# Sketched attention and a GELU layer: the opening in another order

## Chip, cores and metric

The kernel runs on one core of a Trainium2 chip. The metric is the device time of one launch, in microseconds (us). Five engines work beside each other and meet at semaphores: TensorE (PE, matmuls; PEld is its weight load), VectorE (DVE), ScalarE (ACT), GpSimd (POOL) and SyncE (SP, which here issues nearly all transfers).

## What is computed

The reference has two parts. For each of 4 batches and 4 heads, with 1088 tokens of width 32, queries and keys get 64 features each: the products of 8 by 8 sketch values.

```python
def phi(x):
    a = np.einsum('rd,bhsd->bhsr', S1, x)
    b = np.einsum('rd,bhsd->bhsr', S2, x)
    return np.einsum('bhsi,bhsj->bhsij', a, b).reshape(*x.shape[:-1], r * r)
q_p, k_p = (phi(q), phi(k))
kv = np.einsum('bhsf,bhsd->bhfd', k_p, v)
z = np.sum(k_p, axis=2)
num = np.einsum('bhsf,bhfd->bhsd', q_p, kv)
den = np.einsum('bhsf,bhf->bhs', q_p, z)[..., None] + 1e-06
...
h = x @ w_in                                   # x: 4352 x 128, w_in: 128 x 2048
g = 0.5 * h * (1.0 + erf(h * inv_sqrt2))
return (g @ w_out).astype(np.float32)          # w_out: 2048 x 128
```

The quotient num / den, with its heads side by side, is x. The sketches S1 and S2 and the weights w_in and w_out come as 64-bit floats.

## The kernel before, in words

**Tiling.** The 1024 main tokens of a batch make two chunks of 512; the 64 tokens that remain of each batch make one last chunk of 256. There are 9 chunks, numbered from 0. The hidden layer of a chunk is 16 hidden products (`hidden`, L564: 128 rows of w_in by 512 tokens), each followed by a GELU on ScalarE (L571), and then output products with w_out. A 512-column product in 32-bit floats shows as two matmul records of 0.43 us each. The first 8 of the 16 hidden blocks of chunks 0 and 1 use a plain output product (`project`, L692); all later ones use a form with fewer multiplications (`two_products`, L641), for which GpSimd makes sums.

**Order.** The order of instructions on each engine is that of the program's text; nothing reorders it (the loop at the end of the function makes each instruction depend on the one before it on its engine). So an instruction that waits holds up everything behind it on its engine. The opening is written out by hand (L724 to L792). Behind it a loop runs over steps t: step t issues one hidden product, then what `at(t, ...)` has put into its slot, then the output products that are due (`products[t]`, two steps behind their hidden product). Steps 0 to 3 are hidden blocks 0 to 3 of chunk 0, steps 4 to 7 those of chunk 1, then blocks 4 to 7 of each.

**The opening's work for batch 0.**

- *Sketches* (`sketches`, L292): SR, the rounded sketches, is transposed on TensorE (L294). VectorE makes S12 (L295) and sT (L297) of it, GpSimd Srep (L300).
- *Keys*: eight TensorE transposes (L306, `key_turn`), copied by ScalarE to kT (L308); key products with S12 (L350); feature products k_p (L367 on VectorE, L364 on GpSimd, of a copy a_t).
- *The remainder keys*: one transpose (`key_turn_rem`), one product (L374), a copy a_rem on ScalarE (L378), and k_p_rem on VectorE (L379).
- *kv*: `kv_first` (L405) sums over the main tokens, `kv_sum_rem` (L425) adds the remainder. ScalarE copies the sum (kv_T, L431), TensorE transposes it (L435), ScalarE copies it to kz (L439).
- *Queries of chunk 0*: VectorE transposes q (L453). Those of chunk 1: TensorE (L306), with the copy on ScalarE put off (L763). Then per chunk `expand_products` (L462), four `expand_copy` on ScalarE (A_sb, L469) and two `expand_multiply` of two instructions each on VectorE (q_pT, L483).
- *Numerators and denominators of chunks 0 and 1* (`attend_by_token`): small products (L530), then on VectorE denominators (L535), reciprocal (L536) and quotient (x_tok, L538). `turn_x` transposes x_tok on TensorE (L546) and copies it to xT, one half on ScalarE and one on VectorE (L549). xT is what the hidden products read.

**Rounding of weights.** Class `Rounding` makes 32-bit floats of the 64-bit words, piece by piece (pieces end at columns 256, 512, 1024, 1536 and 2048): `low_words` (L250, ScalarE), `fields` (L254 and L256, VectorE), `exponents` (L262, ScalarE), `mantissas` (L270 on VectorE; or L267 on ScalarE and L268 on GpSimd), `signs` (L275, VectorE), `product` (L280, VectorE or GpSimd). `finish` is mantissas, signs and product on VectorE. The tiles in between are taken in turn from pools with two or three buffers each.

**Idle products.** `keep_busy` (L722) issues products of zeros whose result nobody reads.

**Transfers.** SP issues the loads one by one, in the order of the text: keys 0 (two halves), queries 0, values 0 (two halves), key remainders, w_in's first piece, the value remainder, queries 1, two more pieces of weights. The rest (`load_rest`) waits for a one-word memset on GpSimd (L167).

Of the kernel before, what the change touches and what calls it, by code (L numbers as in the profile page):

```python
# [8 lines left out]
FP = mybir.dt.float32  # L9
# [7 lines left out]
def kernel(  # L17
# [56 lines left out]
    def halves(banks):  # L74
        return [banks[:, i] for i in range(2)]

    def hidden_bank():
        return hps.tile([128, CW], FP, name="h_ps")

    def out_bank():  # L80
        return ops.tile([128, CW], FP, name="o_ps")
# [4 lines left out]
    LC = 512  # L86
# [10 lines left out]
    def load_main(eng, n, b, heads=slice(0, H)):  # L97
        eng.dma_start(out=main[n, b][:, heads],
                      in_=src_of[n][b, heads, 0:MAIN, :].rearrange("h (p j) d -> p h j d", j=J))
# [18 lines left out]
    def load_rem(n, b):  # L118
        sp.dma_start(out=rem[n][b // 2 * REM:(b // 2 + 1) * REM, b % 2],
                     in_=src_of[n][b, :, MAIN:S, :].rearrange("h p d -> p h d"))  # L120
# [36 lines left out]
    def load_w_in(i):  # L157
        src, e = words(moe_w_in)
        c0, c1 = pieces[i]
        sp.dma_start(out=landing(w_in_sb[i], e == 2), in_=src[:, c0 * e:c1 * e])  # L160
# [17 lines left out]
    for r in range(2):  # L178
        load_main(sp, "k", 0, slice(r, H, 2))
    load_q(0)  # L180
    for r in range(2):
        load_main(sp, "v", 0, slice(r, H, 2))
    load_rem("k", 0)
    load_rem("k", 2)
    load_w_in(0)
    load_rem("v", 0)
    load_q(1)
# [3 lines left out]
    def load_rest():  # L191

        load_w_out(1, gated=True)
        for i in range(2, len(pieces)):
            load_w_in(i)
            load_w_out(i)
        for b in range(1, B):
            load_turned_k(b)
            load_main(sp, "v", b)
            for c in range(NCH):  # L200
                load_q(b * NCH + c)
            if b == 1:
                for n, b1 in (("k", 1), ("k", 3), ("v", 1), ("v", 2), ("v", 3)):
                    load_rem(n, b1)
        for b in range(B):
            load_rem("q", b)
# [29 lines left out]
    class Rounding:  # L236


        def __init__(self, dst):
            self.dst, self.wide = dst, dst.name in raw  # L240
            if self.wide:
                rows, n = dst.shape
                self.lo, self.hi = raw[dst.name][:, :, 0], raw[dst.name][:, :, 1]
                self.a, self.e, self.r = (mlp.tile([128, LC], U32, name=f"bits_{x}", bufs=2 if x == "r" else 3)[:rows, :n]
                                          for x in "aer")
                self.low, self.m = (mlp.tile([128, LC], FP, name=f"bits_{x}")[:rows, :n] for x in ("low", "m"))

        def low_words(self):
            if self.wide:
# [42 lines left out]
    def sketches():  # L292
        ps = work_bank()
        pe.transpose(ps[:, :2 * R], in_=SR, identity=ident[:2 * R, :2 * R])  # L294
        dve.tensor_mul(out=S12, in0=ps[:, None, :2 * R].broadcast_to([128, H, 2 * R]),  # L295
                       in1=mask4[:, :, None].broadcast_to([128, H, 2 * R]))
        dve.tensor_copy(out=sT, in_=ps[:, :2 * R])  # L297
        for i in range(2):
            src = sT[:, 0:R, None] if i == 0 else sT[:, None, R:2 * R]
            pool.tensor_copy(out=Srep[:, i], in_=src.broadcast_to([128, R, R]))  # L300

    def transposed(ps, name, srcs, copy):

        n = len(srcs) * 128
        for i, s in enumerate(srcs):
            pe.transpose(ps[:, i * 128:(i + 1) * 128], in_=s, identity=ident)  # L306
        t = att.tile([128, n], FP, name=name, bufs=1 if name == "kT_rem" else 2)
        copy(out=t, in_=ps[:, :n])  # L308
        return t

    def four_tokens(n, b, h, c):
        return main[n, b][:, h, c * JC:(c + 1) * JC, :].rearrange("p j d -> p (j d)")
# [12 lines left out]
        for r in range(2):  # L325
            pool.tensor_copy(out=to[rows, :, r, r, :], in_=rem["v"][rows, b % 2, r::2])

    def key_turn(b, r, ps, copy):
        kT[r] = transposed(ps, "kT", [four_tokens("k", b, h, c) for h in (r, r + 2) for c in range(NCH)], copy)

    def key_turn_blocks(b, r):

# [37 lines left out]

        kT["rem"] = transposed(ps[:, 256:], "kT_rem", [rem["k"][:, pair].rearrange("p h d -> p (h d)")], copy)

    def key_features_rem(pair, ps):
        pe.matmul(ps[:, 384:448], lhsT=kT["rem"][:, :128], rhs=S12.rearrange("p h r -> p (h r)"), start=True, stop=True)  # L374
        k_p_rem[pair] = big.tile([128, H, R, R], FP, name=f"k_p_rem{pair}")
        ab = ps[:, 384:448].rearrange("p (h r) -> p h r", r=2 * R)
        a = att.tile([128, H, R], FP, name="a_rem")
        act.copy(out=a, in_=ab[:, :, 0:R])  # L378
        dve.tensor_mul(**spread(k_p_rem[pair], a, ab[:, :, R:2 * R]))  # L379

# [52 lines left out]
    def turn_kv(b, ps, copy):  # L433
        if b == 0:
            pe.transpose(ps[:, :128], in_=kv_T[b], identity=ident)  # L435
        else:
            for rows in (slice(0, 64), slice(64, 128)):
                pe.matmul(ps[rows, :128], lhsT=kv_T[b][:, rows], rhs=ident, start=True, stop=True)
        copy(out=kz[b].rearrange("p c n -> p (c n)"), in_=ps[:, :128])  # L439
# [280 lines left out]
    def keep_busy(n, ps, cols=256):  # L720
        for i in range(n):
            pe.matmul(ps[:, CW - cols:], lhsT=idle[:, 0:128], rhs=idle[:, :cols], start=True, stop=True)  # L722
# [6 lines left out]
    r.exponents()  # L729
    r.finish()  # L730
    key_turn(0, 0, hidden_bank(), by_act)
    key_turn(0, 1, hidden_bank(), by_act)
    sketches()
    keep_busy(1, bank)
    query_turn(0)
    widen_v(0)
    banks = [out_bank(), out_bank()]
# [2 lines left out]
    widen_v(1)  # L740
    widen_v_rem(0)
    expand_products(0)
    w_in = [Rounding(w) for w in w_in_sb[:2]]
    key_turn_rem(0, banks[1], by_dve)
    w_in[0].fields()
    for g in range(2):
        expand_copy(0, g)
    expand_multiply(0, 0)
    kv_bank = out_bank()
    kv_first(kv_bank, 0)  # L750
    expand_copy(0, 2)
    key_features_rem(0, banks[1])
    expand_copy(0, 3)
    expand_multiply(0, 1)
    kv_first(kv_bank, 1)
    keep_busy(1, hidden_bank())
    kv_sum_rem(0, kv_bank)
    w_in[0].exponents()
    take_kv(0, kv_bank, by_act)
    late = []  # L760
    query_turn(1, lambda **a: late.append(a))
    turn_kv(0, kv_bank, by_act)
    by_act(**late[0])  # L763
    w_in[0].signs()
    w_in[1].fields()
    w_in[0].low_words()
    w_in[0].mantissas(by_pool=True)
    load_rest()
    w_in[0].product(pool)
    w_in[1].low_words()  # L770
    w_in[1].exponents()
    banks = [hidden_bank(), hidden_bank()]
    keep_busy(1, banks[0], 128)
    w_out = [Rounding(w) for w in w_out_sb[:2]]
    w_out[0].fields()
    attend_by_token(0, banks)
    expand_products(1)
    bank = out_bank()
    keep_busy(1, bank)
    w_out[0].low_words()  # L780
    for g in range(2):
        expand_copy(1, g)
    w_in[1].mantissas()
    w_in[1].signs()
    w_in[1].product(pool)
    turn_x(0, [hidden_bank(), hidden_bank()])
    keep_busy(1, bank)
    for i in range(2):
        for g in range(2):
            if i:  # L790
                expand_copy(1, 2 + g)
        expand_multiply(1, i)  # L792


    steps = [(n, fi) for f in range(0, USUAL, 4) for n in range(NCH) for fi in range(f, f + 4)]
# [3 lines left out]
    def at(t, f, *a):  # L799
        slots[t].append(lambda: f(*a))  # L800
# [61 lines left out]
    at(17, features_rem, 1)  # L862
    at(18, channel_sums, 4)
    at(18, query_expand, 2)
    at(20, finish_keys, 1)
    at(22, lambda: turn_kv(1, held["kv"], by_act))
    at(23, query_turn, 3)
    at(24, attend, 2)
    for i, t in enumerate((25, 26, 28)):
        at(t, channel_sums, i)  # L870
    for n in range(3, NCHUNK):
# [49 lines left out]
    for t in range(len(steps) + LAG):  # L921
        if t < 4:

            hidden(0, t)
            if t == 0:
                w_out[0].exponents()
                w_out[0].finish()
                w_out[1].fields()
            if t == 3:
                attend_by_token(1, halves(work_banks()), lambda: (w_out[1].exponents(), w_out[1].low_words(),  # L930
                                                                  w_out[1].mantissas(by_pool=True)))
                w_out[1].signs()
                w_out[1].product()
                for u in range(4):
                    for f, *a in products[u]:
                        f(*a)
            continue
        if t == 4:
            turn_x(1, [work_bank(), work_bank()])
            for f, *a in products[t]:  # L940
                f(*a)
        for n in drains[t]:
            drain(n)
        if t < len(steps):
            n, fi = steps[t]
            hidden(n, fi, by_halves=t >= 18 and (n < NMAIN or fi < 5))
        if t < len(steps) and steps[t][0] < NMAIN and steps[t][1] % NB == NB - 1:
            n, b = steps[t][0], steps[t][1] // NB
            if b >= first_block(n):
                token_sums(n, b)  # L950
        for f in slots[t]:
            f()
        for n in done[t]:
            store(n)
        if t != 4:
            for f, *a in products[t]:
                f(*a)
    for n in done[len(steps) + LAG]:
# [40 lines left out]
```

## Time and profile before

| | us |
|---|---|
| median of 4 runs | 274.21 (273.63 to 274.26) |
| the profiled execution, its own time | 273.63 |
| its span in the profile | 271.8 |
| TensorE / VectorE / ScalarE / GpSimd busy | 265.7 / 167.2 / 145.8 / 170.6 |
| hidden products (L564), busy | 140.7 |
| first hidden product of chunk 0 starts | 17.43 |
| first hidden product of chunk 1 starts | 25.67 |
| longest stop of TensorE after that, before L396 | 0.91, ending at 55.41 |

The span is the time from the first instruction of the profile to the last; the execution's own time is longer by what lies around it. Lines such as "L564" are lines of the kernel before, and "x8" counts instructions. The profile's timeline merges neighbours of one kind: its second number runs from the start of the first to the end of the last. The chain that ended last is followed back from the end of the program, at each step to what released the instruction. A matmul's end is modelled, so I go by starts, and by the distance from one start to the next. "Issue" is time in which an engine waited for nothing that the profile shows.

### The profile page before, as it was taken

The numbers are of one execution on the slowest core, as the hardware profiler recorded it, in microseconds if no ns is written. First come the engines' busy times: TensorE is split into PE (matmuls) and PEld (weight loads), VectorE is DVE, ScalarE is ACT, GpSimd is POOL, SyncE is SP. The second block draws the span as 40 slices with busy tenths as digits, with TensorE's granted clock in tenths as the row PEclk, the third lists the DMA queues.
The fourth block names the chain that finished last, engine by engine and source line by source line (L and its number), as shares of the span: only waits on it lengthen the run. The fifth ranks groups of instructions, "written<-read, shape, count | busy, mean of one in ns | idle before, by whom it ended". The sixth has DMA issues, their size and how long they took to land.

```text
span 271.8 us, 5822 instructions
## 1 busy us (share of the span) xinstructions
PE 265.7 (98%) x2326; PEld 137.0 (50%) x2326; DVE 167.2 (62%) x264; ACT 145.8 (54%) x291; POOL 170.6 (63%) x176
## 2 busy tenths in 40 slices
PE   8999999989999999999999999999999999999994
PEld 6755444354454545444445445344444454445794
DVE  5996778543795699679316898488047902760140
ACT  4694766566655633583357533773367344734431
POOL 3331006899987499368875798568866886777400
PEclk9999999999999999999999999999999999999999
DMA  7459373635201100010200000200200020011020
GB/s 211 156 153 364 60 173 65 171 71 144 53 2 18 24 0 2 16 27 0 42 0 2 0 2 2 39 0 2 39 0 2 0 40 4 1 22 19 2 38 20
DMA packets 37915, 13.50 MB, mean 50 GB/s; under 512 B 28288, under 2 KB 37248, under 8 KB 37888
## 3 DMA queue, kind: packets, MB, share of 16 engines
q1 hardware_dynamic: 37648, 13.05, 19.3%
q8 instruction: 18, 0.29, 0.4%
q10 hardware_dynamic: 240, 0.08, 0.1%
q14 instruction: 9, 0.07, 0.1%
HBM read 10.90 MB, written 2.23 MB: 48 GB/s over the span
## 4 chain that ended last, share of the span: by engine, by line
PE 94%; DVE 3%; ACT 2%; issue 0%; POOL 0%; POOLq 0%
PE h_ps L564 43%; PE o_ps L641 31%; PE o_ps L692 5%; PE w_ps L689 3%; PE w_ps L462 3%; PE w_ps L504 2%; PE w_ps L396 1%; PE w_ps L722 1%; ACT A_sb L469 1%; PE w_ps L350 1%; DVE q_pT L483 1%; PE h_ps L306 1%; DVE k_p L367 0%; PE w_ps L425 0%; PE w_ps L530 0%
## 5 line engine op out<-in xcount | busy, mean ns | idle before, releaser
L564 PE MATMUL h_ps<-xT,w_in 128*64 128x512 f32 (+3 forms) x518 | 140.7, 577 | 0.2 <-ACT xT L549 0.2
L571 ACT ACTIVATE block<-h_ps 128x512 f32<-128x512 f32 (+1 forms) x128 | 72.7, 570 | 95.2 <-PE h_ps L564 92.7
L641 PE MATMUL o_ps<-block,w_out 128*64 128x256 f32 x224 | 57.8, 380 | 0.0
L564 PEld LDWEIGHTS h_ps<-xT,w_in 128*64 128x64 f32 (+1 forms) x518 | 42.1, 143 | 30.2 <-issue 10.9
L606 POOL TENSOR_TENSOR bits_low<-block 128x512 f32<-128x512 f32 x28 | 36.6, 1308 | 26.6 <-ACT block L571 26.5
L641 PEld LDWEIGHTS o_ps<-block,w_out 128*64 128x64 f32 x224 | 30.0, 137 | 38.4 <-issue 29.6
L607 POOL TENSOR_TENSOR bits_a<-block 128x512 f32<-128x512 f32 x28 | 36.4, 1302 | 16.7 <-ACT block L571 16.6
L483 DVE TENSOR_TENSOR q_pT<-A_sb,w_ps 64x512 f32<-64x512 f32 x32 | 22.1, 690 | 31.9 <-ACT A_sb L469 31.2
L609 POOL TENSOR_TENSOR bits_m<-block,bits_e 128x512 f32<-128x512 f32 x28 | 36.3, 1295 | 2.2
L608 POOL TENSOR_TENSOR bits_e<-bits_a,block 128x512 f32<-128x512 f32 x28 | 36.1, 1290 | 2.2
L512 DVE RECIPROCAL den<-den 128x512 f32<-128x512 f32 (+1 forms) x7 | 21.9, 3121 | 13.7 <-ACT den L511 13.7
L641 PE MATMUL o_ps<-bits_a,small 128*64 128x256 f32 x112 | 29.0, 382 | 0.0
L641 PE MATMUL o_ps<-bits_m,w_out 128*64 128x256 f32 x112 | 28.8, 379 | 0.0
L641 PE MATMUL o_ps<-block,small 128*64 128x256 f32 x112 | 28.7, 379 | 0.0
L641 PE MATMUL o_ps<-bits_low,small 128*64 128x256 f32 x112 | 28.7, 379 | 0.0
L641 PEld LDWEIGHTS o_ps<-block,small 128*64 128x64 f32 x112 | 15.3, 137 | 18.0 <-issue 12.8
L657 DVE TENSOR_TENSOR sums<-o_ps,sums 64x512 f32<-64x512 f32 x8 | 5.5, 682 | 25.1 <-ACT sums L654 25.1
L469 ACT COPY A_sb<-w_ps 64x512 f32<-64x512 f32 (+1 forms) x36 | 17.6, 557 | 3.4 <-PE w_ps L462 3.3
L516 DVE TENSOR_TENSOR xT<-w_ps,den 32x512 f32<-32x512 f32 (+1 forms) x28 | 18.2, 649 | 1.0
L641 PE MATMUL o_ps<-bits_e,small 128*64 128x256 f32 x112 | 16.8, 379 | 0.0
L692 PE MATMUL o_ps<-g,w_out 128*128 128x512 f32 x32 | 16.4, 599 | 0.1
L511 ACT ACTIVATE den<-w_ps 32x512 f32<-32x512 f32 (+1 forms) x28 | 15.6, 558 | 1.3 <-PE w_ps L504 1.0
(158 smaller groups left out, 323.2 us busy)
## 6 DMA issues: line engine op xcount, KB each, us to landing
block<-in_moe_w_in_dram SPq DMA_DIRECT2D x3, 512.0 KB, 6.8
block<-in_moe_w_out_dram SPq DMA_DIRECT2D x3, 512.0 KB, 10.2
k<-in_k_dram SPq DMA_DIRECT2D x48, 32.0 KB, 1.8
v<-in_v_dram SPq DMA_DIRECT2D x3, 512.0 KB, 4.1
q<-in_q_dram SPq DMA_DIRECT2D x24, 64.0 KB, 3.4
out_dram<-oT SPq DMA_DIRECT2D x24, 64.0 KB, 2.2
k<-in_k_dram SPq DMA_DIRECT2D x2, 256.0 KB, 2.8
q<-in_q_dram SPq DMA_DIRECT2D x2, 256.0 KB, 4.3
```

What stands on the lines that cost most here:

```text
L469: act.copy(out=A[g // 2][F:, g % 2, :width[n]], in_=B_of[n][g // 2][:F, g % 2, :width[n]])
L483: dve.tensor_mul(out=cols[r * F:(r + 1) * F], in0=a[:, :, r::2], in1=b[:, :, r::2])
L512: dve.reciprocal(out=den[:, :W], in_=den[:, :W])
L516: dve.tensor_mul(out=xT[n][rows, :W], in0=banks[h % 2][rows, :W], in1=den[rows, :W])
L564: pe.matmul(ps[rows, :W], lhsT=w[:, rows], rhs=xT[n][:, :W], start=True, stop=True)
L571: act.activation(out=g_of[n, fi][:, :W], in_=ps[:, :W], func=ACT.Gelu)
L606: pool.tensor_sub(out=s[3], in0=a11, in1=a21)
L607: pool.tensor_add(out=s[1], in0=a21, in1=a22)
L608: pool.tensor_sub(out=s[2], in0=s[1], in1=a11)
L609: pool.tensor_sub(out=s[4], in0=a12, in1=s[2])
L641: pe.matmul(acc[n][bank][half * 64:(half + 1) * 64, col:col + HW], lhsT=fixed, rhs=moving, start=opens and e == 0 and name in "4715", stop ...
L692: pe.matmul(o_of[n], lhsT=w_tile(w_out_sb, fi), rhs=g, start=first, stop=final)
```

## The change

The computation is the same. What differs is the order, one engine, one buffer, and three idle products.

- SP issues the second half of the values behind the two key remainders.
- `sketches` runs after six of the eight key transposes; it ran after all eight and was followed by an idle product, which goes.
- The remainder's k_p_rem of batch 0 is made by GpSimd. For that ScalarE copies all 16 sketch values per head instead of 8. (For later batches it stays as it was.)
- The idle products ahead of `kv_sum_rem` and ahead of chunk 0's `turn_x` go.
- The fields of w_in[0] and all other weight rounding move behind chunk 0's q_pT; the steps of the four first pieces of weights are put in another order. The low words of w_out[0] and w_out[1] go into the second half of the tiles that hold those of w_in[0] and w_in[1].
- ScalarE does one A_sb copy of chunk 1 ahead of chunk 0's xT, one behind the second GELU, and VectorE does the second half of chunk 1's q_pT inside step 1.
- w_out[1] is rounded on VectorE alone, ahead of chunk 1's denominators; a part of it was done on GpSimd, and the rest behind them.
- At steps 3 to 5 the output products of chunk 0 come earlier: two ahead of chunk 1's L530, one ahead of its `turn_x`, and one straight behind it, where it was behind two hidden products of chunk 1.
- `finish_keys`, `turn_kv` and `attend` of the next batch move by one step.

```diff
-    for r in range(2):
-        load_main(sp, "v", 0, slice(r, H, 2))
+    load_main(sp, "v", 0, slice(0, H, 2))
     load_rem("k", 0)
     load_rem("k", 2)
+    load_main(sp, "v", 0, slice(1, H, 2))
...
-                self.low, self.m = (mlp.tile([128, LC], FP, name=f"bits_{x}")[:rows, :n] for x in ("low", "m"))
+
+                self.lows = beside.lows if beside else mlp.tile([128, LC], FP, name="bits_low")
+                self.low = self.lows[:rows, n:2 * n] if beside else self.lows[:rows, :n]
+                self.m = mlp.tile([128, LC], FP, name="bits_m")[:rows, :n]
...
         for i, s in enumerate(srcs):
+            if 2 * i == len(srcs):
+                midway()
             pe.transpose(ps[:, i * 128:(i + 1) * 128], in_=s, identity=ident)
...
-        a = att.tile([128, H, R], FP, name="a_rem")
+        both = att.tile([128, H, 2 * R], FP, name="a_rem")
+        if by_pool:
+            act.copy(out=both, in_=ab)
+            pool.tensor_mul(**spread(k_p_rem[pair], both[:, :, 0:R], both[:, :, R:2 * R]))
+            return
+        a = both[:, :, 0:R]
...
-    key_turn(0, 1, hidden_bank(), by_act)
-    sketches()
-    keep_busy(1, bank)
+    key_turn(0, 1, hidden_bank(), by_act, midway=sketches)
...
-    w_in = [Rounding(w) for w in w_in_sb[:2]]
     key_turn_rem(0, banks[1], by_dve)
-    w_in[0].fields()
...
-    key_features_rem(0, banks[1])
+    key_features_rem(0, banks[1], by_pool=True)
     expand_copy(0, 3)
     expand_multiply(0, 1)
     kv_first(kv_bank, 1)
-    keep_busy(1, hidden_bank())
     kv_sum_rem(0, kv_bank)
-    w_in[0].exponents()
+    w_in = [Rounding(w) for w in w_in_sb[:2]]
+    w_out = [Rounding(w_out_sb[0], beside=w_in[0])]
+    w_in[0].low_words()
+    w_in[0].fields()
     take_kv(0, kv_bank, by_act)
     late = []
     query_turn(1, lambda **a: late.append(a))
     turn_kv(0, kv_bank, by_act)
+    w_in[1].low_words()
+    w_in[0].exponents()
     by_act(**late[0])
+    w_in[1].fields()
     w_in[0].signs()
-    w_in[1].fields()
-    w_in[0].low_words()
     w_in[0].mantissas(by_pool=True)
     load_rest()
+    w_out.append(Rounding(w_out_sb[1], beside=w_in[1]))
     w_in[0].product(pool)
-    w_in[1].low_words()
     w_in[1].exponents()
     banks = [hidden_bank(), hidden_bank()]
     keep_busy(1, banks[0], 128)
-    w_out = [Rounding(w) for w in w_out_sb[:2]]
-    w_out[0].fields()
     attend_by_token(0, banks)
     expand_products(1)
-    bank = out_bank()
-    keep_busy(1, bank)
     w_out[0].low_words()
-    for g in range(2):
-        expand_copy(1, g)
     w_in[1].mantissas()
+    expand_copy(1, 0)
+    turn_x(0, [hidden_bank(), hidden_bank()])
+    keep_busy(1, out_bank())
     w_in[1].signs()
     w_in[1].product(pool)
-    turn_x(0, [hidden_bank(), hidden_bank()])
-    keep_busy(1, bank)
-    for i in range(2):
-        for g in range(2):
-            if i:
-                expand_copy(1, 2 + g)
-        expand_multiply(1, i)
+    w_out[0].fields()
+    expand_copy(1, 1)
+    expand_multiply(1, 0)
+    expand_copy(1, 2)
...
-    at(20, finish_keys, 1)
-    at(22, lambda: turn_kv(1, held["kv"], by_act))
+    at(21, finish_keys, 1)
+    at(23, lambda: turn_kv(1, held["kv"], by_act))
     at(23, query_turn, 3)
-    at(24, attend, 2)
+    at(25, attend, 2)
...
             if t == 0:
                 w_out[0].exponents()
+            if t == 1:
                 w_out[0].finish()
+                expand_copy(1, 3)
+                expand_multiply(1, 1)
+                w_out[1].low_words()
                 w_out[1].fields()
             if t == 3:
-                attend_by_token(1, halves(work_banks()), lambda: (w_out[1].exponents(), w_out[1].low_words(),
-                                                                  w_out[1].mantissas(by_pool=True)))
-                w_out[1].signs()
-                w_out[1].product()
+                w_out[1].exponents()
+                w_out[1].finish()
                 for u in range(4):
                     for f, *a in products[u]:
                         f(*a)
+                attend_by_token(1, halves(work_banks()))
+                for f, *a in products[4]:
+                    f(*a)
             continue
         if t == 4:
             turn_x(1, [work_bank(), work_bank()])
-            for f, *a in products[t]:
+            for f, *a in products[5]:
                 f(*a)
...
-        if t != 4:
+        if t > 5:
             for f, *a in products[t]:
                 f(*a)
```

More of the change, by code (lines that the diff above doesn't have):

```diff
@@ L236, with __init__ @@
     class Rounding:
-        def __init__(self, dst):
+        def __init__(self, dst, beside=None):
             self.dst, self.wide = dst, dst.name in raw
@@ L300, in sketches, with transposed @@
             pool.tensor_copy(out=Srep[:, i], in_=src.broadcast_to([128, R, R]))
-    def transposed(ps, name, srcs, copy):
+    def transposed(ps, name, srcs, copy, midway=lambda: None):
         n = len(srcs) * 128
         for i, s in enumerate(srcs):
+            if 2 * i == len(srcs):
+                midway()
             pe.transpose(ps[:, i * 128:(i + 1) * 128], in_=s, identity=ident)
@@ L326, in widen_v_rem, with key_turn @@
             pool.tensor_copy(out=to[rows, :, r, r, :], in_=rem["v"][rows, b % 2, r::2])
-    def key_turn(b, r, ps, copy):
-        kT[r] = transposed(ps, "kT", [four_tokens("k", b, h, c) for h in (r, r + 2) for c in range(NCH)], copy)
+    def key_turn(b, r, ps, copy, midway=lambda: None):
+        kT[r] = transposed(ps, "kT", [four_tokens("k", b, h, c) for h in (r, r + 2) for c in range(NCH)], copy, midway)
     def key_turn_blocks(b, r):
@@ L371, in key_turn_rem, with key_features_rem @@
         kT["rem"] = transposed(ps[:, 256:], "kT_rem", [rem["k"][:, pair].rearrange("p h d -> p (h d)")], copy)
-    def key_features_rem(pair, ps):
+    def key_features_rem(pair, ps, by_pool=False):
         pe.matmul(ps[:, 384:448], lhsT=kT["rem"][:, :128], rhs=S12.rearrange("p h r -> p (h r)"), start=True, stop=True)
```

## The prediction

> **What bounds the kernel now.** I read the page's first part, then the shares of the chain that ended last, then that chain in order of time over the opening, then each engine's timeline up to 32 us. From the page:
>
> ```profile
> PE 265.7 (98%) x2326; PEld 137.0 (50%) x2326; DVE 167.2 (62%) x264; ACT 145.8 (54%) x291; POOL 170.6 (63%) x176
> ...
> PE 94%; DVE 3%; ACT 2%; issue 0%; POOL 0%; POOLq 0%
> ```
>
> TensorE is busy for 98% of the span and 94% of the chain is its. After the opening, a change pays only what it takes from TensorE's stream. The chain in order of time (start, length, what) shows where the opening ends:
>
> ```profile
> 14.67 0.73 POOL bits_m L268
> 15.40 0.04 POOL small L167
> 15.43 0.43 ACT bits_low L250
> 15.86 0.01 issue
> 15.88 1.06 ACT A_sb L469 x2
> 16.93 0.02 issue
> 16.96 0.38 ACT xT L549
> 17.34 0.09 issue
> 17.43 3.83 PE h_ps L564 x8
> 21.26 1.07 PE w_ps L530 x64
> 22.32 1.91 PE o_ps L692 x4
> 24.24 0.44 PE w_ps L546 x4
> 24.68 0.06 issue
> 24.74 1.10 PE o_ps L692 x2
> 25.84 1.72 PE h_ps L564 x4
> ```
>
> Chunk 0's first hidden product starts at 17.43, behind weight rounding (L268, L250) and two copies of A_sb that stand ahead of xT's in ScalarE's queue. Chunk 1's first hidden product starts at 25.84 on the chain; its matmul record starts at 25.67, and I count from records. From there TensorE runs almost without a gap, so the change is worth what it moves the start of that product, plus the products that it has put ahead of it. The timelines of three engines give the rows that set the order before 17.43:
>
> ```profile
> 6.66 0.71 DVE L453 STREAM_TRANSPOSE qT<-q 128x512 f32<-128x512 f32 x1 [0.47 <-DMA q<-in_q_dram]
> 11.44 0.42 DVE L379 TENSOR_TENSOR k_p_rem<-a_rem,o_ps 128x256 f32<-128x256 f32 x1
> 7.97 1.07 POOL L364 TENSOR_TENSOR k_p<-a_t 128x512 f32<-128x512 f32 x1
> 12.01 0.45 PE L425 MATMUL o_ps<-k_p_rem,v_rem_aug 128*64 128x64 f32 x8
> 13.51 1.14 PE L530 MATMUL h_ps<-kz,q_pT 64*64 64x33 f32 x64
> ```
>
> The brackets say what ended an idle time: the query transpose waits for its load.
>
> **Sketches amid the transposes: nothing.** SR is ready at 4.94 (L280 4.66 + 0.28), so its transpose can run at about 5.2, not 5.55, and without the idle product (5.71 to 6.34) the key products (L350) start near 5.8, not 6.34. But the next product, L462 at 7.49, needs qT, whose transpose starts at 6.66 on the landing of q. That load stays third in SP's queue. VectorE then runs qT and three k_p products back to back to 9.23. So half a microsecond is won up to 7.0 and waits at 7.45. Were q to land earlier, up to 0.4 us more would come.
>
> **V's second half behind two remainder loads: nothing.** It lands at 8.03 now; the loads that overtake it are 64 KB, about 0.25 us at the 250 GB/s of that stretch, so 8.3 to 8.5. GpSimd's copy of it (L318) starts at 8.98 behind k_p, and TensorE needs it at 10.29 only. Landing up to 9.6 costs nothing; beyond that it costs one for one. The remainder keys land earlier, but their transpose at 8.59 follows L462 without a wait.
>
> **The remainder's product by GpSimd and the dropped idle product: 0.6 us.** Now a_rem's copy ends at 10.59, VectorE is in q_pT until 11.40, k_p_rem ends at 11.86, L425 runs at 12.01, and an idle product fills 11.38 to 12.0. By GpSimd it may start when the copy of both halves (128x64; L366's 128x64 copies take 0.22, 0.03 more than the 128x32 copy now) is done and seen: 10.70, GpSimd being free from 10.07. This 128x256 spread product has no row. Bounds: 0.53, half of the spread 128x512 row (1.07, L364), and 0.73, the plain 128x256 row (L268). I take 0.62, half way between, because the spread row is the same operation and a fixed part must remain: end 11.32, L425 at 11.42, just after the second L405 group's issue ends at 11.38. The dearer end makes 11.5. So L425 moves from 12.01 to 11.42.
> [...]
>
> **The rest up to the first hidden product.** Each step keeps its distance in the trace of before. kv_T's copy, its transpose and kz's copy: L530 follows L425 by 1.50, at 12.92. qp is ready: VectorE, rid of two fields and k_p_rem, ends the fourth q_pT at about 12.66 (A_sb's fourth copy ends 11.22, two products at 0.72). The denominators follow L530 by 1.19: 14.11. Ahead of them VectorE runs four fields (12.69 to 13.6) and one sign step, which waits for ScalarE's exponents: kz 12.60, low words 12.76, exponents 13.10 to 13.60, so signs 13.65 to 14.08. This new wait just fits; each tenth that ScalarE is late is a tenth on the path. x_tok follows in 1.32: 15.43. qT's copy, now behind two rounding steps, ends at 14.09, so L462 starts 14.15 and is issued by 15.2, ahead of x_tok. The x transposes start at 15.53 (16.18 now). ScalarE has one A_sb copy ahead of xT, not two: 15.94 to 16.31; VectorE's half 16.16 to 16.59. First hidden product: **16.69, against 17.43, a gain of 0.74**. GpSimd's w_in product, 15.3 to 16.0, is in time. The low words' shared tile takes away the wait at 15.43 above.
>
> **From there to chunk 1's first hidden product.** TensorE: four hidden products, the third held by the first GELU (now 17.82 to 18.42), end at 20.3. Before, L530 for chunk 1 came next; now two output products do, to 22.0, L530 to 23.1, one output product, the x transposes, and the fourth output product. What sets the end is VectorE, which now does the rounding of w_out[1] ahead of chunk 1's denominators. From xT's copy at 16.16: signs and two fields to 17.27; q_pT x2 (0.71 each) to 18.7; w_out[0] finish 0.34 + 0.46 + 0.35; q_pT x2 from 19.84 to 21.27; fields 0.53; mantissas 0.34, signs 0.46, product 0.34, so 22.97; denominators, reciprocal and x_tok 1.32: **24.29, against 23.71**. ScalarE's part is in time: its fourth A_sb copy ends 19.78, w_out[1]'s exponents follow the fields at 21.6. TensorE has issued its third output product by 24.0 and waits 0.4. Transposes 24.39, fourth output product 24.83, chunk 1's hidden product 24.83 + 0.93 = 25.76, against 25.67. That is 0.09 later, but the fourth output product (2 x 0.43 = 0.86), which stands behind two hidden products now, is done. **Gain 0.86 - 0.09 = 0.77 us.** Next in line is w_in's 512-column piece, ready 30.5, needed 30.9 instead of 31.7: no wait, but the margin falls from 1.2 to 0.4.
>
> **Keys, their turn and attend one slot later: nothing.** TensorE stands still for 0.91 at 54.5 to 55.41, until VectorE's second q_pT (55.16) and ScalarE's GELU (55.32) free banks. After the change a hidden product stands there, and it needs the same GELU. The same two pieces of work (1.70 and 0.86) end at 57.97 in either order.
>
> **Sum.** The profiled execution took 273.63 with a span of 271.8, and would take 272.86. It lies 0.58 under the median of 274.21, and I carry the difference over: **273.4**.
>
> **Rivals.** (B) *VectorE is the new bound and is later than that.* The stretch from 16.16 to 24.29 holds hardly an idle moment. In its favour: VectorE steps beside GpSimd get longer elsewhere in this trace (a 128x512 sign step 0.69 alone at 29.01, 0.94 at 46.30). Against: GpSimd has only one 0.73 product here. If x_tok comes 0.6 to 0.8 later, the gain is gone: 274.0 to 274.4, at most 274.9. (C) *More comes off.* If the chain is shorter, TensorE runs on from 24.0: 0.4 more, and 0.4 from the key products if q lands early: 272.6 to 273.0. (D) *Slower: TensorE's clock falls.* Three idle products go. An idle 256-column pass was issued every 0.427 before 4 us and in 0.22 at 16.6: half speed until about 5.3. If the clock fell between 11.4 and 16.7, the products there on the path (0.38, 0.43, 0.25, 1.07, 1.07, 0.44, together 3.6) would take twice as long: 273.4 + 3.6 = 277; half of that stretch, 275.2. It decides when an idle time outlasts those that are harmless now; 0.91 at 54.5 was, and I find none over 0.5 here.
> [...]
>
> **Chances.** Forecast 55% (own range 273.1 to 273.8), B 24%, C 12%, D 9%. The measurement tells 0.2%, 0.55 us, from no change: faster is below 273.66, slower above 274.76. Faster: three quarters of the forecast, 42%, and C, 12%: 54%. Same: 13% of the forecast and 19% of B: 32%. Slower: 5% of B and D's 9%: 14%. The range 272.8 to 274.6 takes in most of B and C and leaves D out; GpSimd's price (0.1 either way) and ScalarE's order (0.2) lie inside.
>
> **What would show it.** Right: L453 still at 6.66; L425 near 11.4, L530 near 12.9, first hidden product near 16.7; VectorE without idle time from 16.2 to 24.3; TensorE idle 0.4 ahead of the second x transposes; L396 ahead of its old place by about 0.8. Wrong if L425 waits for GpSimd beyond 11.6, if the sign step ahead of the denominators waits for ScalarE, or if q's landing moves.

## The result, and the profile after

The changed kernel takes **274.76 us** (median of 36 runs, 274.11 to 277.73) against 273.84 for the kernel before (57 runs, 273.07 to 274.53): a ratio of 1.0038, 95% interval 1.0029 to 1.0048. It is slower, where the prediction said 273.4. Each ratio follows the means of the times rather than the medians beside it, so a few late executions move the ratio first. The profiled execution took 274.36 with a span of 272.6. Line numbers are 10 higher than before behind L355 (L574 is the hidden product, L702 the plain output product, L472 `expand_products` and `query_expand`, L493 q_pT, L540 the numerators, L526 `attend`'s last multiplication), and L257, L259, L273, L278 and L283 are fields, fields, mantissas, signs and product.

The page of the changed kernel, first part and shares of the chain:

```profile
PE 265.4 (97%) x2320; PEld 135.9 (50%) x2320; DVE 166.8 (61%) x264; ACT 145.5 (53%) x290; POOL 171.0 (63%) x176
...
PE 93%; DVE 4%; ACT 1%; issue 1%; DVEq 0%
```

TensorE has 0.3 us less to do (the idle products), yet the span is 0.8 longer: TensorE waits more, and VectorE's share of the chain has risen from 3% to 4%. Where, the timelines of VectorE, GpSimd and TensorE in the opening say (start, length, engine, line):

```profile
5.87 0.70 DVE L463 STREAM_TRANSPOSE qT<-q 128x512 f32<-128x512 f32 x1
10.35 0.63 POOL L385 TENSOR_TENSOR k_p_rem<-a_rem 128x256 f32<-128x256 f32 x1 [0.58 <-ACT a_rem L384]
7.69 1.07 POOL L369 TENSOR_TENSOR k_p<-a_t 128x512 f32<-128x512 f32 x1 [0.72 <-ACT a_t L368]
11.03 0.45 PE L435 MATMUL o_ps<-k_p_rem,v_rem_aug 128*64 128x64 f32 x8
12.54 1.14 PE L540 MATMUL h_ps<-kz,q_pT 64*64 64x33 f32 x64
16.42 3.83 PE L574 MATMUL h_ps<-xT,w_in 128*128 128x512 f32 x8 [0.17 <-DVE xT L559]
```

Up to here all went as forecast or better: the query transpose waited for no load this time, GpSimd's product took 0.63 (0.62 forecast), and chunk 0's first hidden product starts at 16.42 (16.69 forecast, 17.43 before). Then the chain that ended last, which ran over TensorE before, runs over VectorE:

```profile
15.04 0.87 DVE bits_m L273
15.90 0.37 DVE xT L559
16.27 0.33 DVE bits_e L278
16.61 0.20 DVE bits_e L257
16.81 1.00 DVE bits_a L259
...
24.40 0.76 DVE x_tok L548 x2
25.16 0.04 issue
25.21 0.66 PE w_ps L556 x4
25.86 0.86 PE o_ps L702 x2
26.72 2.67 PE h_ps L574 x6
```

One step stands out: the second instruction of `w_out[0].fields()` (L259) is on the chain for 1.00. Its timeline record and GpSimd's beside it:

```profile
16.73 1.09 DVE L259 TENSOR_SCALAR bits_a<-small 128x256 uint32<-128x256 uint32 x1
```

```profile
16.68 0.72 POOL L283 TENSOR_TENSOR w_in<-bits_m,bits_e 128x256 f32<-128x256 f32 x1 [1.06 <-DVE bits_e L278]
17.35 0.32 POOL L224 MEMSET v_rem_aug<- 128x256 f32 x1
```

The same instruction takes 0.29 at three other places. Here it starts 0.05 after GpSimd's product of w_in[1] and ends just behind GpSimd's memset. x_tok of chunk 1 is done at 25.15 instead of the forecast 24.29.

The second loss lies 50 us later. `query_expand(3)` in the chain in order of time, before:

```profile
73.14 1.07 PE w_ps L462 x8
```

and after:

```profile
73.37 1.59 PE w_ps L472 x7
```

Half a microsecond more for the same eight products. VectorE's timeline has the reason, before and then after:

```profile
69.03 2.79 DVE L516 TENSOR_TENSOR xT<-w_ps,den 32x512 f32<-32x512 f32 x4
```

```profile
71.00 2.79 DVE L526 TENSOR_TENSOR xT<-w_ps,den 32x512 f32<-32x512 f32 x4
```

These four multiplications are the end of `attend(2)`; they read the two PSUM banks that it took with `work_banks`. Before, they end at 71.82, ahead of `query_expand(3)` at 73.1. After, `attend` runs a step later, they end at 73.79, and the trace's view of L526 names TensorE's weight load at L472 as what waited for it; before, nothing waits there:

```profile
who waited for it (us, times):
  PEld w_ps L472: 0.2, 1
```

The third of the eight products starts at 73.84, just behind VectorE's end. So it is in all five profiles with the new slots (0.05 to 0.06 behind it); in the nine with the old slots VectorE is done 1.2 us ahead of the first product.

**The account.** The time between two milestones hardly varies between executions with the same order there (0.03 at most), so the profiles can be added up. A is the stretch from the first hidden product to the eighth GELU (chunk 1's block 3), B from the eighth to the 34th GELU, which holds the moved slots; from there to the end it is 189.45 in both.

| us | before | forecast | after | after - before |
|---|---|---|---|---|
| first hidden product starts | 17.43 | 16.69 | 16.42 | -1.01 |
| A | 13.59 | 13.56 | 14.73 | +1.14 |
| B | 48.12 | 48.12 | 48.75 | +0.63 |
| last instruction ends | 268.59 | 267.82 | 269.35 | +0.76 |

(The forecast's A: 0.09 later at chunk 1's first hidden product, as forecast, against a start 0.74 earlier, with 0.86 of output product done: 13.59 + 0.83 - 0.86.) The profiled executions are 0.73 apart (274.36 - 273.63), the medians 0.92; what lies between is taken up under "The median" below.

### The profile page after: what moved, and what is told of

It is laid out like the page before. It is cut to its first block, busy times and chain, and to the rows that moved or that the text cites. A ratio compares the mean times of both kernels' runs of the same rounds, so it can differ in the third digit from the quotient of the medians.

```text
span 272.6 us, 5809 instructions
## 1 busy us (share of the span) xinstructions
PE 265.4 (97%) x2320; PEld 135.9 (50%) x2320; DVE 166.8 (61%) x264; ACT 145.5 (53%) x290; POOL 171.0 (63%) x176
## 4 chain that ended last, share of the span: by engine, by line
PE 93%; DVE 4%; ACT 1%; issue 1%; DVEq 0%
PE h_ps L574 42%; PE o_ps L651 31%; PE o_ps L702 4%; PE w_ps L472 3%; PE w_ps L699 3%; PE w_ps L514 2%; PE w_ps L406 1%; PE w_ps L732 1%; PE w_ps L355 1%; PE o_ps L415 1%; DVE q_pT L493 1%; ACT A_sb L479 1%; DVE bits_m L273 1%; DVE x_tok L548 1%; PE h_ps L311 0%
## 5 line engine op out<-in xcount | busy, mean ns | idle before, releaser
L574 PE MATMUL h_ps<-xT,w_in 128*64 128x512 f32 (+3 forms) x518 | 140.6, 577 | 1.0 <-ACT block L581 0.9
L574 PEld LDWEIGHTS h_ps<-xT,w_in 128*64 128x64 f32 (+1 forms) x518 | 41.9, 143 | 32.1 <-issue 8.9
L493 DVE TENSOR_TENSOR q_pT<-A_sb,w_ps 64x512 f32<-64x512 f32 x32 | 22.1, 691 | 32.3 <-ACT A_sb L479 31.6
L526 DVE TENSOR_TENSOR xT<-w_ps,den 32x512 f32<-32x512 f32 (+1 forms) x28 | 18.2, 648 | 1.0
L702 PE MATMUL o_ps<-g,w_out 128*128 128x512 f32 x32 | 16.4, 600 | 0.7 <-DVE w_out L283 0.7
```

Source lines behind the costliest of these rows:

```text
L493: dve.tensor_mul(out=cols[r * F:(r + 1) * F], in0=a[:, :, r::2], in1=b[:, :, r::2])
L526: dve.tensor_mul(out=xT[n][rows, :W], in0=banks[h % 2][rows, :W], in1=den[rows, :W])
L574: pe.matmul(ps[rows, :W], lhsT=w[:, rows], rhs=xT[n][:, :W], start=True, stop=True)
L702: pe.matmul(o_of[n], lhsT=w_tile(w_out_sb, fi), rhs=g, start=first, stop=final)
```

## The experiments

Each was run beside the kernel before, on the same chip as its runs. Ratios are to its runs; medians in us.

**The theory** after this profile: three separate losses. The slots of keys and attend cost 0.6; a VectorE field step beside a GpSimd product costs 0.8; and, since two of the 36 executions took 277.73, TensorE's clock sometimes rises late. **Rivals**: the later opening alone shifts all that follows, with the slots innocent; or VectorE's chain is simply too long, whatever stands beside it.

### Slots back (experiments 1 and 2)

```diff
-    at(21, finish_keys, 1)
-    at(23, lambda: turn_kv(1, held["kv"], by_act))
+    at(20, finish_keys, 1)
+    at(22, lambda: turn_kv(1, held["kv"], by_act))
     at(23, query_turn, 3)
-    at(25, attend, 2)
+    at(24, attend, 2)
```

> The changed kernel with finish_keys, turn_kv and attend of the next batch back at steps 20, 22 and 24. Theory (the loss has two places): attend one step later holds two PSUM banks until VectorE's last xT product, which then ends 0.4 us behind the query products of step 30 that want them; L472 there takes 1.59 us in the changed kernel and 1.07 before. Back in its old slot that stall goes: 0.5 us less than the changed kernel, so about 0.4 us over the kernel before, with L472 at 73.4 us back at 1.07. Rival (the slots are neutral, as the prediction said, and all of the loss is in the opening): the time stays at 0.9 us over the kernel before.

274.42, ratio 1.0045 (1.0016 to 1.0074). Three of the 12 executions lie near 277.1, the profiled one among them; the median of the other nine is 274.07. B is 48.12 again and `query_expand(3)`'s starts spread over 0.55 instead of 1.07.

The other way round, the three new slots in the kernel before:

> The kernel before with nothing but finish_keys, turn_kv and attend moved to steps 21, 23 and 25. Theory (two places): 0.5 to 0.6 us slower than the kernel before, with L462 at 73 us stretched to about 1.6. Rival (slots neutral): no change within 0.2 us. Its opening is that of the kernel before, so its trace also gives a second look at when the query load lands with the old order of transfers: near 6.6 us if that order sets it, anywhere between 5.2 and 6.6 if executions differ by themselves.

274.10, ratio 1.0020 (1.0006 to 1.0034); B is 48.74, the spread 1.07. So by the traces the slots cost 0.62 to 0.63 in either kernel, whatever the opening does. The medians are coarser: they put the slots at 0.28 here, at 0.34 in experiment 1, and at 0.46 and 0.97 in two later pairs (experiments 3 and 4, 6 and 10). The rival that has them innocent falls.

### The field away from GpSimd's product (experiments 3, 4 and 5)

First behind q_pT's first half (the line moved behind `expand_multiply(1, 0)`):

```diff
-    w_out[0].fields()
     expand_copy(1, 1)
     expand_multiply(1, 0)
+    w_out[0].fields()
```

> The changed kernel with the two fields of w_out[0] behind the first two q_pT products of chunk 1, so that they no longer stand beside GpSimd's w_in product. Theory (VectorE's second field, 1.09 us beside that product, is held up by GpSimd): it takes 0.3 us again, VectorE's chain ends about 0.55 us earlier (less than the 0.8 won at the field, since then ScalarE's fourth A_sb copy at 19.9 us is next in line), and the time falls by 0.5 us, to about 0.4 us over the kernel before. Rival (the order itself is too long: the rounding of w_out[1] ahead of chunk 1's denominators sets the end, however fast the fields are): the long field goes, but x_tok of chunk 1 still ends near 25.1 us and the time stays within 0.2 us of the changed kernel.

274.50, ratio 1.0042 (1.0016 to 1.0068), three of 12 near 277.4. The step takes 0.29 again, but A falls only to 14.37: ScalarE's exponents now wait 0.30 for the later fields, and with them the fourth A_sb copy, for which VectorE waits 0.19. The move took away one wait and made part of another; that is half of what separates this A from that of experiment 5 below. With the old slots as well:

> Both of the former edits of the changed kernel: old slots, and the fields of w_out[0] behind two q_pT products. Theory (two places, which add): 1.0 us less than the changed kernel, so 0.1 us either side of the kernel before or slightly below it. Rival (opening alone, or slots alone): no better than the better of the two single edits, 0.4 us over the kernel before.

274.04, ratio 1.0019 (0.9994 to 1.0044), two of 12 near 276.7; A is 14.37, B 48.12: the two add up.

Then ahead of GpSimd's product instead:

```diff
+    w_out[0].fields()
     w_in[1].signs()
     w_in[1].product(pool)
-    w_out[0].fields()
```

with the old slots:

> The changed kernel with the old slots and with the fields of w_out[0] moved ahead of w_in[1]'s signs, so that they run while GpSimd still waits for those signs. Theory (VectorE held up by GpSimd at that field, 0.9 us; slots 0.5 us): the field takes 0.3 us, q_pT of chunk 1 starts 0.8 us earlier against the first hidden product, x_tok of chunk 1 ends about 7.9 us after the first hidden product (8.7 in the changed kernel, 8.4 with the fields behind q_pT), and most executions lie 1.3 us under the changed kernel's, 0.3 to 0.5 us under the kernel before. Some (about one in seven) lie 3 us higher, since the idle product behind the sketches is still gone. Rival (the chain on VectorE is too long anyway): no better than the kernel before.

273.80, ratio 1.0006 (0.9981 to 1.0031), two of 12 near 276.4. The median of the other ten is 273.72, only 0.15 under the kernel before, where 0.3 to 0.5 was expected. A is 13.99, 0.74 less than in the changed kernel. VectorE's and GpSimd's timelines:

```profile
16.78 0.29 DVE L259 TENSOR_SCALAR bits_a<-small 128x256 uint32<-128x256 uint32 x1
16.98 0.42 DVE L278 SCALAR_TENSOR_TENSOR bits_e<-small,bits_r 128x256 uint32<-128x256 uint32 x1
17.43 1.39 DVE L493 TENSOR_TENSOR q_pT<-A_sb,w_ps 64x512 f32<-64x512 f32 x2
```

```profile
17.48 0.72 POOL L283 TENSOR_TENSOR w_in<-bits_m,bits_e 128x256 f32<-128x256 f32 x1 [1.48 <-DVE bits_e L278]
```

The same GpSimd product now runs beside q_pT, which keeps its 1.39. So it is not a neighbour as such that costs, but that instruction beside this one; and 0.74 of the 1.14 lost in A was it.

### The idle product, and the executions near 277 (experiments 6, 7, 11 and 9)

The profiles of the first and third experiment fell on such late executions. Stretches of 3 us of the first experiment (from:to, busy time and number of instructions of each engine, TensorE's granted clock, DMA share, GB/s), and of the changed kernel's profiled execution:

```profile
8.00:11.00 3.00, 3.00 (x23) 1.25 (x21) 1.76 (x4) 1.23 (x4) 2.03 (x4) 1.00 0.89 278
```

```profile
8.00:11.00 3.00, 3.00 (x71) 2.46 (x67) 2.57 (x6) 2.43 (x6) 2.35 (x5) 1.00 0.78 256
```

TensorE is busy throughout in both and issues 23 matmuls in the one, 71 in the other. The same eight products, there and here:

```profile
8.03 2.09 PE L472 MATMUL w_ps<-qT,Srep 32*128 32x512 f32 x8
```

```profile
7.18 1.14 PE L472 MATMUL w_ps<-qT,Srep 32*128 32x512 f32 x8
```

They run at about half speed (2.09 against 1.14). The column of the granted clock says 1.00 all the same; the trace's clock records have full speed from 14.15 in this execution (14.21 in the third experiment), and from 4.9 to 7.4 in all the others. To put back the dropped idle product (two 256-column passes) behind the transposes and sketches, with the two other edits:

```diff
     key_turn(0, 1, hidden_bank(), by_act, midway=sketches)
+    keep_busy(1, bank)
     query_turn(0)
```

> As the former, with the one idle product behind the sketches and key transposes put back (128x256, ahead of the key products). [...] Rival (the executions near 277 come from something else, such as late loads): they still appear, in about 2 of 12.

273.58, ratio 0.9993 (0.9980 to 1.0006), 273.12 to 274.41, none late; the median is 0.29 under the kernel before, but the interval of the ratio takes in 1. I call this the repaired kernel. And the reverse, the idle product alone taken out of the kernel before:

> The kernel before without nothing but the idle product that follows the sketches. Theory (that product decides the clock): most executions are as with the kernel before, or up to 0.3 us faster, and one or two of 12 lie about 3 us higher, with the clock rising near 10.7 or 14.2 us. Rival (the late clock comes from the other two idle products or from the new order): none lies higher than 274.7.

275.29, ratio 1.0018 (0.9996 to 1.0041), in two groups: five executions at 273.25 to 273.75, seven at 275.28 to 275.42. That is more often late than expected (one or two of 12), and by less (1.8 us, not 3). The profiled one was of the early group, and none of the profiles here has a rise near 10.7. Once more, for a profile of the other:

> The kernel before without its idle product behind the sketches, once more, to see the execution times again that fell into two groups 1.8 us apart, near 273.5 and near 275.3 (7 of 12), and if the profile falls into the later group, where its time goes. [...]

273.67 (273.43 to 275.61), ratio 1.0023 (1.0000 to 1.0045): three of eight near 275.4, and the profile again of the early group. So the group is repeated, but its trace was not seen; that it too is a clock rising late is inferred.

The idle product back in the changed kernel, and nothing else:

> The changed kernel with nothing undone but the idle product: it stands again behind the chunk-0 key transposes with the sketches between them. Theory (three causes add up: keys' slots 0.5 us, field beside GpSimd 0.4 to 0.8 us, and a late clock in some executions only where the idle product is missing): this takes away the third alone, so no execution lies about 3 us above the others, and the median stays at 274.2 to 274.6. Rival (the late clock comes from the sketches' new place amid the transposes, not from the idle product): some executions near 277 remain. Rival (the idle product was worth its time to every execution): median at 273.9 or less.

274.73 (274.53 to 275.44, 6 runs), ratio 1.0042 (1.0025 to 1.0058): none late, but a tenth above what I expected, so it buys the typical execution nothing. A is 14.74, B 48.75, as in the changed kernel.

| | executions over 2 us (old order: over 1.5) above the median of the others |
|---|---|
| new order, no idle product (changed kernel, experiments 1, 3, 4, 5) | 12 of 84 |
| new order, idle product back (6, 8, 9, 10, 12) | 0 of 54 |
| old order, idle product (the kernel before, all its executions) | 1 of 167 |
| old order, no idle product (7, 11) | 10 of 20 |

The idle product makes late executions rare, in both orders; the one late execution of the kernel before (277.76) says that it does not rule them out.

### The product on GpSimd, undone in the repaired kernel (experiment 8)

```diff
-    key_features_rem(0, banks[1], by_pool=True)
+    key_features_rem(0, banks[1])
```

> The kernel with swap, old slots and idle product, and with the remainder's k_p_rem on VectorE again. Theory (GpSimd takes that product off VectorE's queue): L435 waits for VectorE about 0.4 us longer than in the kernel with GpSimd, the first hidden product and all behind it come 0.4 us later, so the time is 0.4 us above that kernel. Rival (the remainder's product is hidden either way, since VectorE's chain behind the first hidden product decides): within 0.1 us of that kernel.

274.06, ratio 1.0004 (0.9991 to 1.0016), 0.48 above the repaired kernel's 273.58. The first hidden product starts at 17.74 where the clock rose at 7.04; with the product on GpSimd it started at 17.48 and 17.53 where the clock rose later still (7.29, 7.39). So this part of the change is worth 0.2 to 0.5, as a part of the 0.6 forecast for it and the idle product together.

### The slots in the repaired kernel, and that kernel once more (experiments 10 and 12)

> The changed kernel with the idle product back and the first output field ahead of GpSimd's second weight product, but with the key steps at 21, 23 and 25 as the change has them. Against the kernel with the same two edits and the old slots (273.58 median) theory expects the slots' whole price and nothing else: query_expand(3) spread over 1.0 to 1.1 us from first to last start instead of 0.55, and a median of 274.0 to 274.2. Rival (the slots cost only in the company of the later opening, since the VectorE copies of that stage follow from it): median 273.5 to 273.8.

274.55, ratio 1.0021 (1.0009 to 1.0034). The spread is 1.07 and B 48.75, as expected; the median is higher than expected, its profiled execution having a clock that rose at 7.39 and a first hidden product at 17.53. How much of the median's surplus is such executions is not settled.

> The kernel of the three edits together (idle product back, the output weight's fields ahead of GpSimd's second product, keys and attend in their old slots) once more with more rounds, to tell whether it beats the kernel before. Theory: in the trace it gains 0.54 us up to the first hidden product and gives back 0.40 up to chunk 1's last GELU, so it ends 0.1 to 0.3 us ahead: ratio 0.9990 to 0.9997, none near 277. Rival (the late clock only happened not to show in 12 executions): some executions at 276 or more.

273.62 against 273.61, ratio 1.0001 (0.9987 to 1.0015), none late; the expected gain of 0.1 to 0.3 does not show. The repaired kernel is as fast as the kernel before, and no version here is measurably faster. Its own terms: 0.54 to 0.70 won up to the first hidden product, 0.40 lost in A.

## Why the prediction was wrong, step by step

- **Sketches, V's second half: nothing.** The order held. That q's landing gates qT did not: qT started at 5.87 in the changed kernel, without a wait, and between 5.87 and 6.66 over all profiles. The landing differs by execution, so a gate read off one profile was no fixed point. It worked in the change's favour, by luck as far as the landing goes: L472 starts 0.34 earlier (7.18 against 7.52). A part may be the sketches' new place, which was put at nothing: where q was in time in the old order (experiments 7 and 11), qT still stood behind the sketches until 6.37 and 6.38. No run parts the two.
- **Remainder's product and dropped idle product: 0.6.** GpSimd's product was right (0.63 for 0.62) and so was the order behind it; L435 ran at 11.03. Two things were lumped in one term, though: the idle product ahead of `kv_sum_rem`, free to drop, and the one behind the sketches, whose loss I costed only by what TensorE would otherwise do there. It also kept late executions rare (1 of 167 with it in the old order, 10 of 20 without).
- **First hidden product at 16.69.** Between 16.42 and 17.53 in the changed order (late executions and experiment 8 left out), mostly by when the clock rises; in experiment 4 (a rise at 5.41, a start at 17.08) the numerators' products (L540) also stop for half a microsecond, for no reason that the trace gives. At like rises it starts 0.63 to 0.66 earlier than in the old order (16.89 at 5.99 against 17.55 at 5.97; 17.53 at 7.39 against 18.16 at 7.13) with the idle product in the changed order, and 1.01 earlier without (16.42 against 17.43 at 5.2), of which 0.34 is the earlier L472. So the 0.74 forecast for this stretch was of the right size.
- **"From there to chunk 1's first hidden product": here the forecast failed first.** "Signs and two fields to 17.27" ended at 17.82, by the 0.80 that L259 lost beside GpSimd. Rival B named this very effect and I priced it down because GpSimd had "only one 0.73 product here"; one was enough: the instruction beside it lost 0.80, and the product takes 0.72. With the field moved (experiment 5 and after) the stretch from xT's copy to x_tok's end still takes 8.57, not 8.13: I had added lengths where distances from start to start count: 0.09 to 0.10 is missing at the signs and fields, at w_out[0]'s finish and at the second fields, and 0.17 between w_out[1]'s product and the denominators (0.51 in the repaired kernel, 23.06 to 23.57, where I took the product at 0.34). So A would have been 13.99 even without the collision, and the forecast gain 0.4 smaller.
- **"Keys, their turn and attend one slot later: nothing": here it failed second, by 0.63.** I looked at the stop ahead of kv, which stayed as forecast (0.9, ending 55.5), and asked what starts later. I did not ask what is *released* later: `attend` holds two banks until VectorE's last multiplication, and `query_expand(3)`, which was not moved, wants them. That is 0.52, by the traces; `attend` was never moved alone. The other 0.11 of B lies around kv: the two pieces of work that I had ending alike in either order take 2.72 after (55.50 to 58.22) and 2.57 before (55.41 to 57.98), less 0.04 that the stop ends sooner.
- **Rivals.** B came true: x_tok ended 0.86 later than forecast, where B had 0.6 to 0.8. That this is near is partly luck: the stretch began 0.31 earlier than forecast (15.85 for 16.16) and was 1.17 too long (9.30 for 8.13). Of C, q's early landing came, and TensorE did not run on from 24.0. D had the price of 277 and the wrong event: the clock did not fall, it rose later, and in few executions. That an idle time decides it, as I had it there, no run shows: in the two late profiles TensorE shows no idle time from 2.6 to 14.1. None of the rivals had the slots.
- **The median.** The profiles account for +0.73, the medians for +0.92. The two late executions do not move a median; both profiled executions had an early rise (5.2) and were below their medians, by 0.40 after and 0.21 before. That the changed order loses more with a late rise is possible, since its first hidden product lies up to 1.1 apart between profiles, but was not measured over many executions.

## What to carry to other kernels

When work is moved later, list what it holds (banks, buffers) and who takes them next, not only who waits for its result: the unmoved taker paid here. A chain on one engine is added up by distances from start to start, and each step on it is looked at beside what runs on GpSimd in the new order. And an idle product is not judged by what it displaces in one profile: look at the spread of many executions with and without it. A step that another engine holds up costs only if what stands behind it would have been ready: of the two that GpSimd held up here, one cost 0.74 and the other nothing.

## What the runs showed of the hardware

**VectorE beside GpSimd.** A field step of 0.29 took 1.08 to 1.09 in all three profiles (the changed kernel, experiments 1 and 9) in which it started just after a GpSimd product with two inputs from SBUF, and 0.29 in all others of the new order (in the old order, 0.32 to 0.39 where a GpSimd copy ran beside it). The mantissa step L273, with two SBUF inputs, took 0.85 to 0.96 where it started early in GpSimd's product of w_in[0] (nine profiles of the new order), ending 0.27 to 0.29 behind that product in all nine; in the old order it started later in that product and took 0.56. It took 0.42 where it started 0.12 before the product's end (experiment 4):

```profile
15.62 0.42 DVE L273 SCALAR_TENSOR_TENSOR bits_m<-bits_a,bits_low 128x256 f32<-128x256 uint32 x1
16.51 0.42 DVE L559 COPY xT<-h_ps 128x256 f32<-128x256 f32 x1 [0.48 <-PE h_ps L556]
```

It stands just ahead of xT's copy, yet this hold cost nothing: in experiment 4 the copy waited for TensorE and started 0.66 behind the x transposes (15.85 to 16.51), and 0.66 to 0.67 in the nine others too. q_pT, with one input in PSUM, kept its time: 1.39 for two beside GpSimd's product of w_in[1] (experiment 5), 1.41 for the next two, with GpSimd idle.
The hold fits GpSimd's work in size: the field step lasted from 16.73 to 17.82, GpSimd's product ran to 17.40 and its memset to 17.67. Why these two steps take longer beside it and q_pT does not, no run here shows.

**TensorE's clock at the start.** It rose between 4.90 and 7.39 in twelve profiles and at 14.15 and 14.21 in two. In the two late ones TensorE shows no idle time from 2.6 to 14.1. In two of the early ones (experiments 7 and 11) it was idle for 0.48 between 2.6 and 7.0, and the clock rose all the same.
What keeps the clock from rising when TensorE shows no idle time, no run here settles; why the idle product helps stays open.
